# Startup order, named banks and the joints of pairs in an attention and expert kernel

## The chip, the core and the metric

The kernel runs on one core of a Trainium2 chip. The metric is the device time of one execution in microseconds (us). The core's engines run side by side, each through its own queue of instructions in a fixed order: TensorE (PE, matmuls; PEld its weight loads), VectorE (DVE), ScalarE (ACT), GpSimd (POOL) and SyncE (SP), which issues all the DMAs here. Results of TensorE go to PSUM, to which this kernel gives six tiles A0, A1, B0, B1, C0 and C1 (banks, called A, B and C in the rows) and the tile `psa`.

## The reference

Attention over chunks of 64 tokens, then a layer of four experts on its output. All is float32.

```python
scores = scale * q_c @ k_c.T          # 8 batches, 8 heads, 9 chunks of 64, head size 64
scores = scores - max(scores)
attn = exp(scores); attn = attn / (sum(attn) + 1e-09)
x = (attn @ v_c), reshaped to 4608 tokens x 512
p = domain_probs / (domain_probs.sum(-1) + 1e-09)
out = 0
for e in range(4):
    h = maximum(x @ w1[e], 0)          # 512 -> 1024
    out += p[:, e] * (h @ w2[e])       # 1024 -> 512
```

## The kernel before

**Numbers.** A float32 operand is split into a high part (a cast, on ScalarE) and a low part (the rest, on VectorE or GpSimd: L268 for x and weights, L463 and L637 for hidden values). A product is three matmuls for each k: high by high, low by high, high by low (L455). In the rows, xh and xl are the parts of x, wf a weight of the first layer (the name is also used for other buffers), hfh and hfl parts of hidden values and of second-layer weights.

**Tiling.** The tokens are nine blocks of 512. Block 0 goes alone, the other eight in four pairs. The hidden dimension and the experts are cut so that a block or a pair needs eight passes. Passes 0 to 7 are block 0: the startup is pass 0, `plain_pass` the rest. Passes 8 to 15 are the first pair (`first_pair_pass`), 16 to 39 the other three (`first_later_pass` is pass 16, `later_pass` the rest). A pass of a pair does its two layers not with eight products but with seven each, of sums and differences of the operands: p1 to p7 of a group. Groups g and h are the first layer, a and b the second, and the second layer of one pass is woven with the first layer of the next. The sums of x (`Tokens.sum1` to `sum4`, L405 and L420) are made at the last pass of the pair before: these are the joints of pairs, passes 23 to 24 and 31 to 32. The sums of the weights in the first pair (`w2.sum1` to `sum4`) are made in its passes, and `keep` stores their parts to memory for the pairs that follow. The sums of the hidden values (`sc.sum`, L628) have their high parts by L634 and low parts by L637. L683 adds products of the second layer to `acc`; L517 copies a product out of a bank (s), L656 and L622 combine such copies.

**Order.** Nothing is scheduled automatically. Each engine takes its instructions in the order in which the program issues them. A pass issues its products one after the other and behind step i the functions in `at[i]`, filled with `add(at, i, ...)`. What is handed on to the next pass stands in a list `late`. A bank is taken by name or, without a name, in turn. Who takes a tile that is still in use waits for the last user; this holds for a whole tile.

**The startup.** It loads the first block, keeps TensorE busy with matmuls of zeros (`keep_warm`, L857, into the tile `idle`), computes the attention of four tiles of 128 tokens (scores L815, softmax L182 to L187, weights L190 to L195, transposes L826, values L839, parts of x L265 and L268) and mixes in the first hidden products (`plain_hidden`). The sums of the softmax are also written to the tile `idle`:

```python
a_norm(es[t], sc[t], idle[:, 1, t * 2 * HG : (t + 1) * 2 * HG])
```

In the rows `idle` is called psa.

## Time and profile before

| | us |
|---|---|
| median of 3 runs | 1561.61 |
| lowest and highest | 1560.61, 1562.14 |
| the profiled execution | 1560.53 |
| its span | 1558.7 |
| TensorE busy in it | 1527.6 (98%) |
| VectorE busy | 918.0 (59%) |
| GpSimd busy | 883.2 (57%) |
| ScalarE busy | 574.3 (37%) |

The profile is one execution; the span is from its first to its last instruction. TensorE is near its whole span at work, so the waits that it still has lie in a few places, and the rows below are taken from there. The mean granted clock is 0.995 of full speed.

### The profile page before, as it was taken

The page shows a single profiled execution, that of the slowest core. Times are in us where ns is not written, and L with a number is a line of the kernel's source. Part 1 is how long each engine was busy: PE and PEld are TensorE (multiplying, and loading weights), DVE is VectorE, ACT ScalarE, POOL GpSimd, SP SyncE. Part 2 cuts the span into 40 slices and gives each one's busy share as a digit, 9 for nine tenths or more (in the row PEclk, how much of TensorE's full clock was granted, in tenths as well). Part 3 has the DMA queues.
Part 4 walks back from the last instruction along what each step waited for, and adds up shares of the span by engine and source line. Part 5 has one row for each costly group of instructions (what it writes and reads, how often), then busy time and mean ns, then how long its engine had stood idle before and what let it go on. Part 6 is the DMA issues. An engine that isn't in the chain of part 4 may idle for free.

```text
span 1558.7 us, 23407 instructions
## 1 busy us (share of the span) xinstructions
PE 1527.6 (98%) x8854; PEld 1240.8 (80%) x8854; DVE 918.0 (59%) x1288; ACT 574.3 (37%) x999; POOL 883.2 (57%) x664
## 2 busy tenths in 40 slices
PE   7999999999999999999999999999999999999998
PEld 5877877888888887888887778888887788888886
DVE  4444454444444456676777855666768745666665
ACT  3333444444433433333333434333333343333332
POOL 2333477676665715555555665555556755555554
PEclk8999999999999999999999999999999999999999
DMA  5345237877676676666665567676665576666654
GB/s 191 105 129 154 83 119 267 288 264 238 233 247 216 217 256 190 204 221 217 205 215 193 191 198 237 205 220 211 216 199 192 174 236 198 203 199 198 205 195 132
DMA packets 164831, 314.16 MB, mean 202 GB/s; under 512 B 14176, under 2 KB 79984, under 8 KB 164720
## 3 DMA queue, kind: packets, MB, share of 16 engines
q1 hardware_dynamic: 164720, 312.68, 61.8%
q8 instruction: 70, 1.15, 0.3%
q14 instruction: 41, 0.34, 0.1%
HBM read 244.39 MB, written 68.23 MB: 201 GB/s over the span
## 4 chain that ended last, share of the span: by engine, by line
PE 87%; DVE 4%; POOL 4%; DMA 3%; ACT 2%; issue 1%; SPq 0%; DVEq 0%; ACTq 0%; POOLq 0%
PE A L455 42%; PE C L455 25%; PE B L455 15%; PE psa L168 1%; PE psa L139 1%; POOL hfl L637 1%; PE psa L159 1%; DVE xl L268 1%; DMA w<-hfh 1%; DMA w<-wf 1%; POOL wf L268 1%; DMA wraw<-in_w 1%; DVE acc L683 1%; POOL xl L268 1%; PE psa L769 1%
## 5 line engine op out<-in xcount | busy, mean ns | idle before, releaser
L637 POOL TENSOR_TENSOR hfl<-wraw,hfh 128x512 fp32r<-128x512 f32 x288 | 388.8, 1369 | 209.0 <-ACT hfh L634 207.2
L455 PE MATMUL A<-xh,wf 128*128 128x512 f32 (+1 forms) x1112 | 382.9, 391 | 2.2 <-ACT s L517 2.0
L455 PE MATMUL A<-hfh,wf 128*128 128x512 f32 x768 | 271.1, 394 | 1.0 <-DVE acc L683 1.0
L634 ACT CAST hfh<-wraw 128x512 fp32r<-128x512 f32 x288 | 174.1, 622 | 216.6 <-POOL wraw L628 53.3
L455 PEld LDWEIGHTS A<-xh,wf 128*128 128x128 f32 x1112 | 208.2, 188 | 47.7 <-ACT s L517 2.9
L517 ACT COPY s<-A 128x512 f32<-128x512 f32 x192 | 112.8, 587 | 356.5 <-PE A L455 352.2
L455 PE MATMUL A<-xl,wf 128*128 128x512 f32 (+1 forms) x556 | 215.5, 388 | 2.3 <-POOL xl L268 2.3
L455 PE MATMUL C<-xh,wf 128*128 128x512 f32 (+1 forms) x584 | 201.4, 392 | 0.0
L455 PEld LDWEIGHTS A<-hfh,wf 128*128 128x128 f32 x768 | 144.2, 188 | 32.1 <-DVE acc L683 2.5
L683 DVE TENSOR_TENSOR acc<-A,acc 128x512 f32<-128x512 f32 x174 | 119.3, 685 | 79.6 <-PE A L455 78.6
L455 PE MATMUL A<-hfl,wf 128*128 128x512 f32 x384 | 149.8, 390 | 0.0
L455 PE MATMUL C<-hfh,wf 128*128 128x512 f32 x384 | 135.7, 395 | 3.2 <-DVE acc L683 2.9
L268 POOL TENSOR_TENSOR hfl<-wraw,hfh 128x512 fp32r<-128x512 f32 x64 | 85.9, 1370 | 85.5 <-ACT hfh L265 81.2
L455 PE MATMUL B<-xh,wf 128*128 128x512 f32 (+1 forms) x384 | 127.0, 384 | 1.3 <-DVE acc L751 1.3
L455 PEld LDWEIGHTS C<-xh,wf 128*128 128x128 f32 x584 | 109.6, 189 | 23.2
L268 POOL TENSOR_TENSOR wf<-wraw,wf 128x512 fp32r<-128x512 f32 x70 | 91.3, 1329 | 60.6 <-ACT wf L265 58.4
L455 PEld LDWEIGHTS A<-xl,wf 128*128 128x128 f32 x556 | 104.4, 188 | 23.8 <-POOL xl L268 3.1
L628 POOL TENSOR_TENSOR wf<-wraw,wf 128x512 f32<-128x512 f32 x23 | 29.7, 1293 | 165.1 <-DVE wf L622 165.1
L455 PE MATMUL C<-xl,wf 128*128 128x512 f32 (+1 forms) x292 | 113.3, 390 | 1.3 <-POOL xl L268 1.3
L683 DVE TENSOR_TENSOR acc<-C,acc 128x512 f32<-128x512 f32 x90 | 62.0, 690 | 58.9 <-PE C L455 54.6
L637 POOL TENSOR_TENSOR hfl<-wf,hfh 128x512 fp32r<-128x512 f32 x48 | 71.1, 1481 | 35.5 <-ACT hfh L634 35.5
L455 PEld LDWEIGHTS C<-hfh,wf 128*128 128x128 f32 x384 | 72.1, 188 | 20.1 <-DVE acc L683 4.9
(179 smaller groups left out, 2729.9 us busy)
## 6 DMA issues: line engine op xcount, KB each, us to landing
wf<-w SPq DMA_DIRECT2D x336, 512.0 KB, 4.1
wraw<-in_w SPq DMA_DIRECT2D x128, 256.0 KB, 3.6
w<-wf SPq DMA_DIRECT2D x112, 256.0 KB, 4.1
qk_in<-in_qk SPq DMA_DIRECT2D x32, 512.0 KB, 4.7
v_in<-in_v SPq DMA_DIRECT2D x32, 256.0 KB, 4.6
w<-hfl SPq DMA_DIRECT2D x32, 256.0 KB, 2.4
w<-hfh SPq DMA_DIRECT2D x32, 256.0 KB, 2.8
w<-hfh SPq DMA_DIRECT2D x48, 128.0 KB, 2.6
```

The lines of the kernel that those rows point to most:

```text
L139: nc.tensor.matmul(s["sc"][half, c, j], lhsT=s["x"][rows, g, 0, h], rhs=s["x"][rows, g, 1, h], start=True, stop=True,)
L159: nc.tensor.transpose(ps[:, j], s["e"][:, j].rearrange("p c k -> p (c k)"), ident)
L168: nc.tensor.matmul(av[half, c, j], lhsT=s["v"][rows, 2 * j + odd], rhs=s["pt"][rows, j, half], start=True, stop=True,)
L268: eng.tensor_tensor(out=t[1], in0=src, in1=t[0].bitcast(F32), op=ALU.subtract)
L455: nc.tensor.matmul(out, lhsT=lhs(k, a), rhs=rhs(k, b), start=first and i == 0, stop=last and i == len(parts) - 1, skip_group_check=not (fi ...
L517: nc.scalar.copy(out=t, in_=self.a)
L628: (eng or nc.vector).tensor_tensor(out=self.values[place, k], in0=self.values[a, k], in1=self.values[b, k], op=op)
L634: nc.scalar.copy(out=self.part(name, 0)[:, k], in_=self.values[name, k])
L637: (eng or nc.gpsimd).tensor_tensor(out=self.part(name, 1)[:, k], in0=self.values[name, k], in1=self.part(name, 0)[:, k].bitcast(F32), op=A ...
L683: nc.vector.tensor_tensor(out=acc[key], in0=src, in1=acc[key], op=ALU.add)
L769: nc.tensor.transpose(out_ps, acc[pair + 1, m + NK * s][:, j * P : (j + 1) * P], ident)
```

## The change

It has five parts. The startup gets an early Exp on one element, more matmuls of zeros, another order of the tiles' steps, and named banks. The last plain pass and the first pair get other banks for tiles (`TILE_BANKS`), and the first pair's pass 8 makes the parts of w2's sums later. Pass 16 makes the parts of t2 one step later. At the joints, x's sums move to other steps and partly to GpSimd. The low part of x's t4 is issued earlier in the next pass, and that of b22 is made on VectorE.

```diff
-WAITS = {"loads": 12, "softmax": 8}
+WAITS = {"loads": 12, "softmax": 14, "copy": 3}
...
-    TILE_BANKS = ("A0", "C0", "B0", "A1", "C1", "B1", "A1", "C1")
+    TILE_BANKS = ("A0", "B0", "C0", "A1", "C1", "B1", "A1", "C1")
...
-        sc[t] = bank().rearrange("p (h s) -> p h s", s=C)
+        sc[t] = bank(("A0", "A1", "C0", "C1")[t]).rearrange("p (h s) -> p h s", s=C)
...
-        w = bank().rearrange("p (j s) -> p j s", s=P)
+        w = bank(("B0", "B0", "B1", "B0")[t]).rearrange("p (j s) -> p j s", s=P)
...
-        av[t] = bank().rearrange("p (j s) -> p j s", s=P)
+        av[t] = bank(("B1", "A0", "A1", "B1")[t]).rearrange("p (j s) -> p j s", s=P)
...
         x_alloc(0)
+
+        nc.scalar.activation(out=small.tile([P, 1], F32, name="first"), in_=zeros[:, :1], func=AF.Exp)
         keep_warm(WAITS["loads"])
         start_scores(0)
         start_scores(1)
         keep_warm(WAITS["softmax"])
         start_softmax(0)
+        start_softmax(1)
         start_weights(0)
-        start_softmax(1)
-        for f, k in QUADS[:3]:
+        for f, k in QUADS[:2]:
             w1_split(f, k, nc.gpsimd)
         start_transpose(0)
-        w1_split(1, 1, nc.gpsimd)
+        keep_warm(WAITS["copy"])
         start_weights(1)
+        for f, k in QUADS[2:]:
+            w1_split(f, k, nc.gpsimd)
+        start_transpose(1)
         start_values(0)
         start_x(0)
-        start_transpose(1)
-        start_scores(2)
         start_values(1)
         start_x(1)
+        start_scores(2)
+        start_scores(3)
+        first = [0, 1]
         start_softmax(2)
         w_load(1, 0, 1, 0)
         w_load(1, 0, 1, 1)
         w2_split(0, 0)
-        start_scores(3)
-        first = [0, 1]
-        plain_hidden(0, first, order=RHS_LO_LAST)
+        start_softmax(3)
         start_weights(2)
+        plain_hidden(0, first, order=RHS_LO_LAST, name="B0")
         w2_split(0, 1)
-        plain_hidden(1, first, order=RHS_LO_LAST)
-        start_softmax(3)
+        plain_hidden(1, first, order=RHS_LO_LAST, name="B1")
         w2_split(1, 0)
-        plain_hidden(2, first, order=RHS_LO_LAST)
+        plain_hidden(2, first, order=RHS_LO_LAST, name="A0")
+        start_weights(3)
         start_transpose(2)
-        start_weights(3)
         w2_split(1, 1)
-        plain_hidden(3, first, order=RHS_LO_LAST)
+        plain_hidden(3, first, order=RHS_LO_LAST, name="C0")
         start_values(2)
         start_x(2)
         norm_probs()
-        o = tiles(0, 0, range(NT))
+        o = tiles(0, 0, range(NT), ("A0", "C0", None, None))
...
-        o = tiles(0, n, range(NT))
+        o = tiles(0, n, range(NT), ("C0", "C1", "A1", "B1") if ahead_of else None)
...
-            add(at, begin_w2 + 1 + i, lambda name=name: w2.hi(name), lambda name=name: w2.lo(name))
-            add(at, begin_w2 + 5 + i, lambda name=name: w2.keep(n, name))
+            later = 9 if begin_w2 else 1
+            add(at, later + i, lambda name=name: w2.hi(name), lambda name=name: w2.lo(name))
+            add(at, later + 4 + i, lambda name=name: w2.keep(n, name))
...
-            add(at, begin_w2 + 9 + i, lambda name=name: w2.hi(name), lambda name=name: w2.lo(name))
-            add(at, begin_w2 + 13 + i, lambda name=name: w2.keep(n, name))
+            later = 18 if begin_w2 else 9
+            add(at, later + i, lambda name=name: w2.hi(name), lambda name=name: w2.lo(name))
+            add(at, later + 4 + i, lambda name=name: w2.keep(n, name))
...
-        put(10, "t2", 0)
+        put(11, "t2", 0)
...
-        late = []
+        late, x_low = [], []
...
-            add(at, 0, x.sum1)
-            add(at, 4, x.sum3)
-            add(at, 7, x.sum2_apart)
+            add(at, 5, x.sum1)
+            add(at, 8, lambda: x.sum3(nc.gpsimd), lambda: x.sum2_apart(nc.gpsimd))
...
+            x_low = [lambda: x.lo("t4", nc.gpsimd)]
             late = [
-                (0, lambda: x.hi("b22")), (0, lambda: first_load(pair + 2)),
-                (7, lambda: x.lo("t4", nc.gpsimd)), (7, lambda: x.lo("b22", nc.gpsimd)),
+                (0, lambda: x.hi("b22")), (0, lambda: first_load(pair + 2)), (5, lambda: x.lo("b22")),
             ]
...
-        add(at, 4, lambda: sc.sum("t4", 1, nc.gpsimd))
+        add(at, 4, *x_low, lambda: sc.sum("t4", 1, nc.gpsimd))
```

In pass 8 `begin_w2` is 5, so w2's parts s1 and s2 went in at steps 6 and 7 and go in at 9 and 10, s3 and s4 at 14 and 15 and now 18 and 19. The last argument of `tiles` and the `name` of `plain_hidden` only say which bank is taken.

VectorE in the startup, the softmax of tiles 0 and 1 before the change (A is the bank with the scores of a tile, m its maxima, psa the tile `idle`):

```order
L182 TENSOR_REDUCE m_291<-A_249 128x8
L184 TENSOR_TENSOR A_249<-A_249,m_291 128x512
L190 TENSOR_REDUCE psa<-A_249 128x8
L191 TENSOR_SCALAR psa<-psa 128x8
L193 RECIPROCAL z_298<-psa 128x8
L195 TENSOR_TENSOR e<-A_249,z_298 128x512
L182 TENSOR_REDUCE m_301<-A_266 128x8
L184 TENSOR_TENSOR A_266<-A_266,m_301 128x512
L190 TENSOR_REDUCE psa<-A_266 128x8
L191 TENSOR_SCALAR psa<-psa 128x8
```

The same rows of VectorE with the change:

```order
L182 TENSOR_REDUCE m_299<-A_251 128x8
L184 TENSOR_TENSOR A_251<-A_251,m_299 128x512
L182 TENSOR_REDUCE m_303<-A_268 128x8
L184 TENSOR_TENSOR A_268<-A_268,m_303 128x512
L190 TENSOR_REDUCE psa<-A_251 128x8
L191 TENSOR_SCALAR psa<-psa 128x8
L193 RECIPROCAL z_310<-psa 128x8
L195 TENSOR_TENSOR e<-A_251,z_310 128x512
L190 TENSOR_REDUCE psa<-A_268 128x8
L191 TENSOR_SCALAR psa<-psa 128x8
```

The maxima of tile 1 now stand ahead of tile 0's sum (L190), and the two sums follow one another.

VectorE at the first joint, in pass 23, before the change (L405 and L420 are x's sums, xraw the pair's x, e and pt the sums kept apart):

```order
L405 TENSOR_TENSOR qk_in<-xraw 128x1024
L683 TENSOR_TENSOR acc_5805<-B_8127,acc_5805 128x512
L656 TENSOR_TENSOR B_8137<-B_8137,s_8119 128x512
L622 SCALAR_TENSOR_TENSOR wraw<-B_8137,s_5524 128x512
L405 TENSOR_TENSOR xraw<-xraw 128x2x512
L683 TENSOR_TENSOR acc_5865<-C_8163,acc_5865 128x512
L683 TENSOR_TENSOR acc_5887<-A_8101,acc_5887 128x512
L420 TENSOR_TENSOR e<-xraw,qk_in 128x512
L420 TENSOR_TENSOR pt<-xraw,qk_in 128x512
L683 TENSOR_TENSOR acc_5887<-C_8163,acc_5887 128x512
```

With the change, from the row that follows L628 on:

```order
L683 TENSOR_TENSOR acc_5816<-B_8136,acc_5816 128x512
L656 TENSOR_TENSOR B_8146<-B_8146,s_8128 128x512
L622 SCALAR_TENSOR_TENSOR wraw<-B_8146,s_5535 128x512
L683 TENSOR_TENSOR acc_5876<-C_8171,acc_5876 128x512
L405 TENSOR_TENSOR qk_in<-xraw 128x1024
L683 TENSOR_TENSOR acc_5898<-A_8112,acc_5898 128x512
L683 TENSOR_TENSOR acc_5898<-C_8171,acc_5898 128x512
```

Of the four sums one stays. It now stands behind the first L683 that reads bank C, where L405 of xraw stood ahead of it, and ahead of the two L683 that follow; the other three are gone from this engine.

GpSimd in the same pass with the change (before it, the last L628 followed the second L637 directly):

```order
L628 TENSOR_TENSOR wraw<-wraw 128x512
L637 TENSOR_TENSOR hfl_8134<-wraw,hfh_8132 128x512
L405 TENSOR_TENSOR xraw<-xraw 128x2x512
L420 TENSOR_TENSOR e<-xraw,qk_in 128x512
L420 TENSOR_TENSOR pt<-xraw,qk_in 128x512
L628 TENSOR_TENSOR wf_8252<-wraw,wf_8252 128x512
L637 TENSOR_TENSOR hfl_8299<-wraw,hfh_8297 128x512 x2
```

The three sums stand ahead of the sum of the hidden values L628.

GpSimd at the start of the next pass, 24, before the change (xl_8427 is the low part of x's t4, xl_8451 that of b22):

```order
L637 TENSOR_TENSOR hfl_8326<-wraw,hfh_8324 128x512
L637 TENSOR_TENSOR hfl_8364<-wf_8241,hfh_8362 128x512
L628 TENSOR_TENSOR wraw<-wraw 128x512
L637 TENSOR_TENSOR hfl_8469<-wraw,hfh_8467 128x512
L268 TENSOR_TENSOR xl_8427<-xraw,xh_8426 128x1024
L268 TENSOR_TENSOR xl_8451<-xraw,xh_8450 128x1024
L628 TENSOR_TENSOR wf_8581<-wraw,wf_8581 128x512
```

And with the change, where xl_8438 is the low part of t4:

```order
L637 TENSOR_TENSOR hfl_8393<-wraw,hfh_8391 128x512
L637 TENSOR_TENSOR hfl_8480<-wraw,hfh_8478 128x512
L637 TENSOR_TENSOR hfl_8337<-wraw,hfh_8335 128x512
L637 TENSOR_TENSOR hfl_8375<-wf_8252,hfh_8373 128x512
L268 TENSOR_TENSOR xl_8438<-xraw,xh_8437 128x1024
L628 TENSOR_TENSOR wraw<-wraw 128x512
L637 TENSOR_TENSOR hfl_8480<-wraw,hfh_8478 128x512
```

The low part of t4 went up past L628 and one L637; the other one is gone from this engine.

## Rows read from the trace of the kernel before

**Rows 1.** Windows: span, busy us (instructions) by engine, granted clock, DMA
```profile
13.40:20.20 6.80, 3.73 (x42) 2.88 (x42) 3.13 (x7) 3.74 (x8) 4.56 (x4) 0.50 0.72 245
...
593.70:597.10 3.40, 3.40 (x9) 2.64 (x8) 2.32 (x4) 1.51 (x3) 2.44 (x3) 0.50 0.19 75
...
850.00:906.00 56.00, 51.85 (x222) 40.77 (x221) 44.32 (x57) 21.26 (x33) 40.20 (x24) 1.00 0.61 201
...
0.00:1559.00 1559.00, 1527.65 (x8854) 1240.80 (x8854) 918.03 (x1288) 574.27 (x999) 883.15 (x664) 0.99 0.62 202
```

**Rows 2.** TensorE's waits: line, releaser, us in total, times, longest
```profile
PE C L455 <- DVE acc L683: 2.9, 2, 1.6
...
PE A L455 <- POOL xl L268: 2.3, 2, 1.2
...
PE A L455 <- ACT s L517: 2.0, 1, 2.0
...
PE A L455 <- DVE hfl L463: 1.6, 1, 1.6
...
PE C L455 <- POOL xl L268: 1.3, 2, 0.7
...
PE B L455 <- DVE acc L751: 1.3, 1, 1.3
...
PE C L455 <- DVE hfl L463: 0.7, 3, 0.3
```

**Rows 3.** Timeline of the startup: start, us, engine, line, operation, idle before
```profile
9.15 1.90 PE L857 MATMUL psa<-s 128*128 128x512 bf16 x8
...
9.18 1.28 ACT L187 ACT_TABLE_LOAD   x1 [9.18 <-DVE A L184]
...
11.16 0.70 DVE L190 TENSOR_REDUCE psa<-A 128x8 f32<-128x512 f32 x1 [2.06 <-ACT A L187]
...
13.18 0.89 PE L826 MATMUL B<-ident,e 128*128 128x128 f32 x4 [2.13 <-DVE e L195]
...
23.08 1.22 PE L455 MATMUL B<-xh,wf 128*128 128x256 f32 x8
...
28.71 0.63 PE L826 MATMUL C<-ident,e 128*128 128x128 f32 x4 [1.06 <-DVE e L195]
...
33.98 1.98 PE L839 MATMUL A<-s,ws 64*64 64x64 f32 x32 [3.21 <-issue]
...
35.89 1.11 PE L826 MATMUL B<-ident,pt 128*128 128x128 f32 x4
...
39.89 1.15 PE L839 MATMUL C<-s,ws 64*64 64x64 f32 x32
```

**Rows 4.** Timeline where tile 0 of pass 7 starts, TensorE and VectorE
```profile
214.32 0.39 PE L455 MATMUL A<-hfh,hfh 128*128 128x512 f32 x1
214.55 0.39 PE L455 MATMUL A<-hfl,hfh 128*128 128x512 f32 x1
...
214.43 1.41 DVE L463 SCALAR_TENSOR_TENSOR hfl<-C,hfh 128x512 fp32r<-128x512 f32 x2
```

**Rows 5.** Timeline of pass 16's start, ScalarE and VectorE
```profile
592.73 0.58 ACT L517 COPY s<-A 128x512 f32<-128x512 f32 x1
...
596.09 0.69 DVE L622 SCALAR_TENSOR_TENSOR wraw<-A,ws 128x512 f32<-128x512 f32 x1 [0.72 <-PE A L455]
```

**Rows 6.** Timeline of the first joint, VectorE and GpSimd
```profile
854.26 1.64 DVE L405 TENSOR_TENSOR xraw<-xraw 128x1024 f32<-128x1024 f32 x1
...
854.76 2.27 POOL L628 TENSOR_TENSOR wraw<-wraw 128x512 f32<-128x512 f32 x1
...
865.26 1.30 POOL L628 TENSOR_TENSOR wf<-wraw,wf 128x512 f32<-128x512 f32 x1 [5.82 <-DVE wf L622]
```

**Rows 7.** Timeline of the next pass's start, ScalarE and GpSimd
```profile
899.51 0.59 ACT L517 COPY s<-A 128x512 f32<-128x512 f32 x1 [1.11 <-PE A L455]
...
899.73 4.71 POOL L268 TENSOR_TENSOR xl<-xraw,xh 128x1024 fp32r<-128x1024 f32 x2
```

More of the change, by code (lines that the diff above doesn't have):

```diff
@@ L402, in __init__, with less @@
                     setattr(self, f"b{k + 1}{s + 1}", x[:, rows, toks])
-        def less(self, name, a, b, out):
-            nc.vector.tensor_tensor(
+        def less(self, name, a, b, out, eng=None):
+            (eng or nc.vector).tensor_tensor(
                 out=out, in0=getattr(self, a), in1=getattr(self, b), op=ALU.subtract
@@ L414, in sum2, with sum2_apart @@
             self.less("t2", "b22", "t1", self.b22)
-        def sum2_apart(self):
+        def sum2_apart(self, eng):
             self.t2 = [att.tile([P, SUB], F32, name=name) for name in ("e", "pt")]
             for k, t in enumerate(self.t2):
-                nc.vector.tensor_tensor(out=t, in0=self.b22[:, k], in1=self.t1[:, k], op=ALU.subtract)
+                eng.tensor_tensor(out=t, in0=self.b22[:, k], in1=self.t1[:, k], op=ALU.subtract)
         def sum4_apart(self):
@@ L432, in split2, with sum3 @@
                 split(nc.vector, t, [part[:, k] for part in xt[i]])
-        def sum3(self):
-            self.less("t3", "b22", "b12", self.b12)
+        def sum3(self, eng=None):
+            self.less("t3", "b22", "b12", self.b12, eng)
         def sum4(self):
@@ L479, in h_part, with plain_hidden @@
         return [t[:, k] for t in hs[s, i]]
-    def plain_hidden(f, tiles, alloc=True, order=BY_BLOCK):
+    def plain_hidden(f, tiles, alloc=True, order=BY_BLOCK, name=None):
         cols = slice(tiles[0] * P, (tiles[-1] + 1) * P)
@@ L484, in plain_hidden @@
             h_alloc(0, f)
-        out = bank()[:, : cols.stop - cols.start]
+        out = bank(name)[:, : cols.stop - cols.start]
         product(
@@ L1176, in later_pass @@
             add(at, i, f)
-        second_half(at, ahead[0])
+        second_half(at, ahead[0], ahead[2:])
         add(at, 12, lambda: sc.sum("t3", 0, nc.gpsimd))
@@ L1223, in later_pass, with second_half @@
                 f()
-        return (sc, left), late
-    def second_half(at, sc):
+        return (sc, left, *x_low), late
+    def second_half(at, sc, x_low=()):
         add(at, 0, lambda: sc.sum("t2", 1))
```

## Prediction

> **What bounds the kernel now.** I read the windows first [rows 1]. Over the whole run TensorE is busy 1527.65 of 1559 us, so nothing but its own waits and its clock can be won. Next came the table of what TensorE waits for [rows 2]. Its waits are few and each has a place: the startup, the step from block 0 to the first pair (about 222 to 249 us), one at 593 us, and the two joints of pairs (about 850 to 906, and the same again from 1182). One thing about these numbers: in a steady run a 512-column matmul starts every 0.23 us while its row lasts 0.39 [rows 4], so a wait between two such rows is 0.16 longer than its idle figure. I add this below. Last came the timeline at each place, to see what a wait's releaser itself had waited for.
>
> In the startup TensorE idles 2.13 us ahead of the transposes of tile 0, 1.06 ahead of those of tile 2 and 3.21 ahead of the values of tile 2 [rows 3]. While the granted clock is down, work takes longer: the window from 13.4 to 20.2 us was granted 0.50 [rows 1], the lower level (1.2 GHz); it was granted just behind the wait of 2.13, which ends at 13.18. The values of tile 2, after the wait of 3.21, took 1.98 us, those of tile 3 only 1.15; transposes took 1.11 at 35.89 and 0.63 at 28.71 [rows 3].
>
> **A, the startup.** The early Exp takes the table load (1.28 us, 9.18) out of tile 0's chain. I cost that at nothing, because of what the sum at 11.16 is: it writes its result into the tile `idle` (psa in the rows), the same tile into which the warm matmuls write, and the order makes it follow the last of them. Before, eight of them end at 11.05 (9.15 + 1.90), just ahead of the sum, whose row names the Exp as what came last [rows 3]. The change makes them fourteen. At 0.24 us each (1.90 for 8) they end near 12.4, so tile 0's sum moves from 11.16 to about 12.5, and its transposes, 2.02 us behind the sum in the rows, from 13.18 to about 14.5. After them (0.63) come three more warm matmuls (0.7), and tile 1's sum now follows those: about 15.8, transposes of tile 1 about 17.9. Then transposes 0.63, values of two tiles and scores of two tiles at about 1.1 each: plain hidden 0 at about 22.9 against 23.08, a gain of 0.2 only.
>
> The gain is behind it. The softmax of tiles 2 and 3 is issued ahead of the hiddens and the weights of tile 2 ahead of hidden 0, so the waits of 1.06 and 3.21 should go: 4.3. The low clock that follows the second of them goes too: 0.83 on the values, 0.48 on the transposes, 1.3 together. A new wait comes: the transposes of tile 2 take bank B1, which hidden 1 has just filled, and wait for its low part, which stands on VectorE behind the weights of tile 2; I estimate 0.6, one short VectorE instruction. So −0.2 − 4.3 − 1.3 + 0.6 = −5.2. Against this stands one more low stretch: TensorE still waits about 2.1 twice (12.4 to 14.5, 15.8 to 17.9), and the wait of 2.13 in the rows was followed by 0.50 from 13.4 on. If the stretch falls on the transposes of tile 1 and the values of tile 0, it costs 0.48 + 0.83 = 1.3. I take it: **−3.9**, bounds −2.5 and −6.
> The Trainium skill, "TensorE: Matmul & The Clock Gate", Part 1, says that the clock follows how busy the engine has been lately. The windows agree. By that rule the longer warm run might as well keep the clock up, and the startup would then give 5.2, not 3.9.
>
> **B, the banks between passes 7 and 8.** The wait of 1.3 for VectorE's `acc` add on bank B (1.43 with the 0.16) goes, since the last tiles of block 0 no longer hold B0. But tile 0 now takes C0, in which hidden 2 still lies: its low part, the first of two in a row, ends near 215.1 (214.43 + half of 1.41), and TensorE starts the tile at 214.32 [rows 4]. The new wait is about 0.8. Sum **−0.6**, bounds +0.8 (the old wait only moves to another bank) and −1.4.
>
> **C, the sums of w2 later in pass 8.** The wait of 1.6 for `hfl` on bank A (1.76) comes from the activations of the hiddens, which stand on ScalarE behind casts of w2's sums. With those casts three to four steps later the activation waits for its bank alone; I leave 0.25 for the rest of the chain, an estimate: **−1.5**, bounds 0 and −1.76. What is moved past: the casts, GpSimd's low parts and the stores that `keep` queues on SP. These stores are first read a pair later, and GpSimd's queue gets the same work three steps later; I cost that at nothing. If that cover fails, one low part on GpSimd is late, 1.3 [rows 6], and C is nearly gone, which is its lower bound.
>
> **D, the first pair's tile banks.** Three waits on C for `hfl`, 0.7 together, with 0.16 each 1.2, in passes 8, 9 and 14: the second tile takes B0 instead of C0, and they go. **−1.2**, bounds 0 and −1.2.
>
> **E, put t2 a step later in pass 16.** TensorE waits 2.0 (2.16) for a COPY on ScalarE at 592.73 [rows 5], which stands behind a cast that itself waited for VectorE. Behind the wait a window of 3.4 us had the clock 0.50, and nine matmuls were started in it [rows 1], for which 0.23 each would be 2.0: 1.4 lost. With the cast behind the COPY, the COPY still needs its own bank; about 0.9 us of wait is left (its own 0.58 and the ways there and back), which would probably not bring the clock down. That gives up to 2.16 + 1.4 − 0.9 = 2.7. But the next step needs bank A from VectorE's L622, at 596.09 in the rows, and the high part that is now later; a wait of some 1 to 2 us comes there instead. **−1.0**, bounds 0 and −2.7.
>
> **F, x's sums away from VectorE at the joint.** Product a3 waits for `acc<-C` [rows 2], which stands in VectorE's queue behind L405 at 854.26 (1.64) [rows 6]. That L405 goes to GpSimd; the one that stays follows behind this `acc<-C`, ahead of later ones that TensorE does not yet want. So both waits (2.9 together, 3.2 with 0.16 each) go. GpSimd gets the three sums, as one of 1024 columns and two of 512. A 512-column sum takes 1.30 there when nothing disturbs it, and L268 of 1024 columns 2.36 (4.71 for 2) [rows 6, 7], so 5.0 us. GpSimd was idle 5.82 us ahead of 865.26 [rows 6], so they lie beside TensorE's work. **−3.2**, bounds −2 and −3.2.
> L628 at 854.76, beside VectorE's L405 with two SBUF inputs, took 2.27, and the same form at 865.26 took 1.30 [rows 6]. At that ratio the sums take 8.7, and the 2.9 past the gap delay L628 and its casts. What VectorE runs in the gap reads a PSUM bank each time, so I go by 1.30.
> The Trainium skill, "SBUF — State Buffer", section "SBUF: two separate sides", says that a VectorE operation with two SBUF inputs and a GpSimd operation hold a common port pair one at a time, each for its whole length. The two rows agree, and it speaks against this part: by it, any such VectorE operation that remains in the gap adds its length.
>
> **G, x's low parts.** The waits for `xl` (2.3 and 1.3 in all, four of them over both joints, 4.24 with 0.16 each) go: the low part of t4 is issued ahead, and that of b22 on VectorE. The price is a new queue. On GpSimd the low part of t4 (2.36) now stands ahead of sum L628, so the cast that reads the sum on ScalarE is about 2.4 later, and the COPY at 899.51 behind that cast too [rows 7]. The COPY can be some 1 us late before g4 wants its bank; I estimate a wait of 0.75 to 1.9 each time and take 1.3: 4.24 − 2.6 = **−1.6**, bounds 0 and −2.8.
>
> **The sum:** −3.9 − 0.6 − 1.5 − 1.2 − 1.0 − 3.2 − 1.6 = −13.0. The profiled execution took 1560.53 us (span 1558.7), 1.1 below the median of the runs. On the median 1561.61 this gives **1548.6 us**.
>
> **The rivals.**
> 1. The startup gains nothing. For it: both waits of 2.1 stay, and the warm matmuls delay the sums more than the table load saved. Against it: the two later waits lose their cause. Without A: 1552.5.
> 2. The joints' waits only move (F and G come to nothing): the sums take 8.7, and the COPY waits behind the cast. For it: the 2.27 at 854.76. Against it: VectorE's work in the gap. 1548.6 + 4.8 = 1553.4.
> 3. The clock does not fall in the startup, and E gives all its 2.7: 1548.6 − 1.3 − 1.7 = 1545.6.
> 4. The other side: GpSimd becomes the bound at the joints. It is busy 40.2 of 56 us there [rows 1]; with the sums at 8.7 that is 49. It decides if a product needs one of GpSimd's low parts before the queue has recovered: then the sums' 8.7 stands on the path at both joints, 17.4, and F and G are lost: 1548.6 + 4.8 + 17.4 = 1570.8. Against it: 7 us are left, and the first reader of a sum is issued ten steps later.
>
> **How the numbers follow.** My forecast gets 0.44, rival 1 0.17, rival 2 0.12, rival 3 0.19, rival 4 0.04. The forecast's own terms move it by about 3 either way. The range 1544 to 1553.5 holds the forecast nearly whole with rivals 1, 2 and 3. What a measurement of this kernel can tell from no change is about 0.2%, 3.1 us; rivals 1 to 3 are all faster by more. Several terms at their poor bounds at once would end within it: the last 0.04. Slower is rival 4: 0.04.
>
> **What would show it.** Right: transposes of tile 0 near 14.5 and tile 0 of block 0 near 31.5 (a row of 512 columns out of `hfh,hfh`), no wait of 3 us in the startup; no wait for `acc` on B between passes 7 and 8, one below 1 us for C0 at the first tile of pass 7; no `acc` wait on C and no `xl` wait at the joints, but one for a COPY of L517 near 900; GpSimd's three sums between 857 and 866 in about 5 us. Wrong: a clock of 0.50 in more of the startup than one stretch, sums of over 2 us each on GpSimd, or a new wait of over 2 us behind the COPY.

## The result and the profile after

| | before | after |
|---|---|---|
| median, us | 1561.32 (4 runs) | 1546.62 (4 runs) |
| lowest and highest | 1560.61, 1562.14 | 1546.44, 1547.34 |
| profiled execution | 1560.53 | 1546.54 |
| its span | 1558.7 | 1544.8 |
| TensorE busy in it | 1527.6 | 1524.5 |

The ratio is 0.9907, with a 95% interval from 0.9889 to 0.9924: 14.7 us less. The forecast was 1548.6, 13.0 less.

What TensorE waits for in the changed kernel behind the startup (line, releaser, us in total, times, longest):

```profile
PE A L455 <- ACT s L517: 3.7, 3, 1.5
...
PE B L455 <- POOL hfl L637: 1.2, 1, 1.2
...
PE C L455 <- DVE hfl L463: 0.7, 1, 0.7
...
PE A L455 <- DVE wraw L622: 0.6, 1, 0.6
PE A L455 <- DVE hfl L463: 0.6, 1, 0.6
```

Of the rows of [rows 2] those for `acc` on C, for `xl` and for `acc` on B are gone. The three waits for `hfl` on C are gone too; the one that stands there now is the first tile of pass 7, which takes C0. The wait of 1.6 for `hfl` on A is gone, and the 0.6 that stands there now comes 30 matmuls later. New are also 1.2 for GpSimd's `hfl`, 0.6 for L622, and two of the three waits for a COPY. In the startup the wait of 2.13 for the weights of tile 0 stays and one as long for those of tile 1 is new; those of 1.06 and 3.21 [rows 3] are gone, and with them one of 3.06 for the copy (L830) of tile 0, which those rows do not show.

Where the time came from is best seen by following the same instruction through both traces. These are starts of the same instruction in the two profiled executions, in us (L749 and L751 take a tile of block 0 or of the first pair into `acc` on VectorE, L517 is a COPY on ScalarE):

| place | before | after | after less before | since the last row |
|---|---|---|---|---|
| L749 of tile 0, block 0 | 40.00 | 34.61 | −5.39 | −5.39 (A) |
| L751, first tile of pass 7 | 221.80 | 216.44 | −5.36 | 0.03 |
| L751, its last tile | 229.97 | 223.77 | −6.20 | −0.84 (B) |
| L749, tile 0 of pass 8 | 257.15 | 249.83 | −7.32 | −1.12 (C) |
| L517, first of pass 10 | 315.63 | 307.43 | −8.20 | −0.88 (D) |
| L517, first of pass 16 | 576.08 | 567.38 | −8.70 | −0.50 (D) |
| L517, in pass 18 | 652.76 | 643.71 | −9.05 | −0.35 (E) |
| L517, pass 23 | 850.96 | 841.95 | −9.01 | 0.04 |
| L517, behind a3 | 866.41 | 855.50 | −10.91 | −1.90 (F) |
| L517, pass 24 | 908.69 | 897.13 | −11.56 | −0.65 (G) |
| L517, pass 30 | 1150.50 | 1138.94 | −11.56 | 0.00 |
| L517, second a3 | 1191.65 | 1178.42 | −13.23 | −1.67 (F) |
| L517, pass 33 | 1267.57 | 1253.71 | −13.86 | −0.63 (G) |

The row of pass 8 holds two things that happen to cancel: its L749 came 0.45 late in VectorE's own queue (the next one is 7.77 earlier than before), and the first of D's three waits lies ahead of it. Followed by TensorE's own matmuls (L455), C is −1.0 and D −1.5.

The startup after, in the same columns as [rows 3]:

```profile
8.90 3.19 PE L857 MATMUL psa<-s 128*128 128x512 bf16 x14
...
9.34 0.58 ACT L187 ACTIVATE A<-A 128x512 f32<-128x512 f32 x1 [7.10 <-DVE A L184]
...
12.21 0.70 DVE L190 TENSOR_REDUCE psa<-A 128x8 f32<-128x512 f32 x1 [1.65 <-PE psa L857]
...
14.23 0.63 PE L826 MATMUL B<-ident,e 128*128 128x128 f32 x4 [2.13 <-DVE e L195]
...
17.64 1.09 PE L826 MATMUL B<-ident,pt 128*128 128x128 f32 x4 [2.13 <-DVE pt L195]
...
18.66 1.97 PE L839 MATMUL B<-s,qk_in 64*64 64x64 f32 x32
...
23.36 1.21 PE L455 MATMUL B<-xh,wf 128*128 128x256 f32 x8
...
28.07 0.66 PE L826 MATMUL B<-ident,e 128*128 128x128 f32 x4
...
31.58 0.48 PE L455 MATMUL A<-hfh,hfh 128*128 128x512 f32 x1
```

The first row of tile 0 of block 0, the last of these, was before:

```profile
36.66 0.78 PE L455 MATMUL B<-hfh,hfh 128*128 128x512 f32 x1
```

The fourteen warm matmuls end at 12.09 (8.90 + 3.19), and tile 0's sum follows at 12.21, with PE as what it waited for, though its Exp was done at 9.92. The transposes come at 14.23 and 17.64, both with a wait of 2.13. The low clock falls within the second: the values of tile 0 take 1.97. From hidden 0 on there is no wait of note: 23.36 to 31.58 at tile 0 of block 0, where before it was 23.08 [rows 3] to 36.66.

The windows (columns as in [rows 1]) show the clock at the lower level, 1.2 GHz, for one stretch of the startup (before there were two, of 6.8 and 3.4 us), and both engines that share the work of a joint:

```profile
17.10:20.50 3.40, 2.86 (x38) 2.56 (x40) 0.39 (x1) 0.59 (x1) 1.47 (x2) 0.50 0.38 128
838.00:894.00 56.00, 53.82 (x234) 43.01 (x233) 45.93 (x57) 22.64 (x36) 44.09 (x27) 1.00 0.61 199
```

GpSimd is busy 44.09 of 56 us there, VectorE 45.93. GpSimd's three sums lie in its gap, and 0.64 of the gap is left ahead of L628 (where 5.82 had been, [rows 6]):

```profile
848.78 2.40 POOL L405 TENSOR_TENSOR xraw<-xraw 128x1024 f32<-128x1024 f32 x1
...
851.13 1.31 POOL L420 TENSOR_TENSOR e<-xraw,qk_in 128x512 f32<-128x512 f32 x1
...
852.40 1.31 POOL L420 TENSOR_TENSOR pt<-xraw,qk_in 128x512 f32<-128x512 f32 x1
...
854.35 1.30 POOL L628 TENSOR_TENSOR wf<-wraw,wf 128x512 f32<-128x512 f32 x1 [0.64 <-DVE wf L622]
```

They took 5.0 us, as estimated. What VectorE keeps of x's sums, L405, ran ahead of them, beside GpSimd's L628 at 844.51, which took 2.29 there instead of 1.30.

The wait of 0.6 for `hfl` on A in pass 8 comes from a load:

```profile
244.13 0.62 ACT L265 CAST wf<-wraw 128x512 fp32r<-128x512 f32 x1 [3.15 <-DMA wraw<-in_w]
...
246.02 0.50 PE L455 MATMUL A<-hfh,hfh 128*128 128x512 f32 x1 [0.59 <-DVE hfl L463]
```

The cast on ScalarE waited 3.15 for the load of a weight. The activation that makes the hidden values stands behind it (244.65), VectorE's low part behind that (245.28), and the product behind that. The new wait of the next pass of the joint, 24:

```profile
884.37 2.31 DVE L268 TENSOR_TENSOR xl<-xraw,xh 128x1024 fp32r<-128x1024 f32 x1
...
885.53 3.40 POOL L268 TENSOR_TENSOR xl<-xraw,xh 128x1024 fp32r<-128x1024 f32 x1
...
888.89 1.28 POOL L628 TENSOR_TENSOR wraw<-wraw 128x512 f32<-128x512 f32 x1
...
890.73 0.58 ACT L517 COPY s<-A 128x512 f32<-128x512 f32 x1
...
891.36 0.50 PE L455 MATMUL A<-xh,wf 128*128 128x512 f32 x1 [1.47 <-ACT s L517]
```

The low part of t4 on GpSimd takes 3.40, not the 2.36 of [rows 7], since it starts while VectorE's low part of b22 runs; L628 stands behind it, the COPY behind the cast of that sum, and TensorE waits 1.47.

### The profile page after: what moved, and what is told of

Its sections match the earlier page's. It is cut to its first block, busy times and chain, and to the rows that moved or that the text cites. A ratio compares the mean times of both kernels' runs of the same rounds, so it can differ in the third digit from the quotient of the medians.

```text
span 1544.8 us, 23430 instructions
## 1 busy us (share of the span) xinstructions
PE 1524.5 (99%) x8863; PEld 1239.6 (80%) x8863; DVE 915.7 (59%) x1284; ACT 574.8 (37%) x1000; POOL 888.5 (58%) x668
## 4 chain that ended last, share of the span: by engine, by line
PE 78%; POOL 3%; DVE 2%; ACT 1%; issue 1%; DMA 0%; DVEq 0%; SPq 0%; POOLq 0%; ACTq 0%
PE A L455 41%; PE C L455 22%; PE B L455 12%; POOL hfl L637 2%; PE psa L168 1%; PE psa L139 1%; DVE xl L268 1%; PE psa L159 1%; PE psa L769 1%; DVE acc L683 1%; POOL wraw L628 0%; POOL xl L268 0%; DVE wraw L628 0%; ACT hfh L634 0%; ACT xh L265 0%
## 5 line engine op out<-in xcount | busy, mean ns | idle before, releaser
L637 POOL TENSOR_TENSOR hfl<-wraw,hfh 128x512 fp32r<-128x512 f32 x288 | 386.1, 1360 | 207.6 <-ACT hfh L634 205.7
L455 PE MATMUL A<-xh,wf 128*128 128x512 f32 (+1 forms) x1112 | 382.4, 390 | 3.9 <-ACT s L517 3.7
L455 PE MATMUL A<-hfh,wf 128*128 128x512 f32 x768 | 271.2, 394 | 1.6 <-DVE acc L683 1.0
L455 PEld LDWEIGHTS A<-xh,wf 128*128 128x128 f32 x1112 | 207.8, 188 | 49.8 <-ACT s L517 5.5
L517 ACT COPY s<-A 128x512 f32<-128x512 f32 x192 | 112.7, 587 | 347.2 <-PE A L455 343.0
L455 PE MATMUL A<-xl,wf 128*128 128x512 f32 (+1 forms) x556 | 214.8, 387 | 0.0
L455 PE MATMUL C<-xh,wf 128*128 128x512 f32 (+1 forms) x584 | 201.1, 391 | 0.0
L455 PEld LDWEIGHTS A<-hfh,wf 128*128 128x128 f32 x768 | 144.2, 188 | 33.1 <-DVE acc L683 2.5
L683 DVE TENSOR_TENSOR acc<-A,acc 128x512 f32<-128x512 f32 x174 | 119.3, 686 | 77.3 <-PE A L455 76.4
L455 PE MATMUL A<-hfl,wf 128*128 128x512 f32 x384 | 149.7, 390 | 0.0
L455 PE MATMUL C<-hfh,wf 128*128 128x512 f32 x384 | 135.4, 394 | 0.2
L268 POOL TENSOR_TENSOR hfl<-wraw,hfh 128x512 fp32r<-128x512 f32 x64 | 86.0, 1371 | 83.4 <-ACT hfh L265 79.8
L455 PEld LDWEIGHTS C<-xh,wf 128*128 128x128 f32 x584 | 109.1, 188 | 23.2
L455 PE MATMUL B<-xh,wf 128*128 128x512 f32 (+1 forms) x384 | 126.9, 383 | 0.0
L268 POOL TENSOR_TENSOR wf<-wraw,wf 128x512 fp32r<-128x512 f32 x70 | 91.4, 1331 | 55.9 <-ACT wf L265 53.6
L455 PEld LDWEIGHTS A<-xl,wf 128*128 128x128 f32 x556 | 104.3, 188 | 20.7
L628 POOL TENSOR_TENSOR wf<-wraw,wf 128x512 f32<-128x512 f32 x23 | 29.8, 1294 | 156.3 <-DVE wf L622 156.3
L455 PE MATMUL C<-xl,wf 128*128 128x512 f32 (+1 forms) x292 | 112.8, 388 | 0.0
L683 DVE TENSOR_TENSOR acc<-C,acc 128x512 f32<-128x512 f32 x90 | 62.1, 691 | 60.7 <-PE C L455 54.8
L637 POOL TENSOR_TENSOR hfl<-wf,hfh 128x512 fp32r<-128x512 f32 x48 | 71.2, 1483 | 35.5 <-ACT hfh L634 35.5
L455 PEld LDWEIGHTS C<-hfh,wf 128*128 128x128 f32 x384 | 72.1, 188 | 16.3 <-DVE acc L683 1.1
```

What stands on the lines that cost most here:

```text
L268: eng.tensor_tensor(out=t[1], in0=src, in1=t[0].bitcast(F32), op=ALU.subtract)
L455: nc.tensor.matmul(out, lhsT=lhs(k, a), rhs=rhs(k, b), start=first and i == 0, stop=last and i == len(parts) - 1, skip_group_check=not (fi ...
L517: nc.scalar.copy(out=t, in_=self.a)
L628: (eng or nc.vector).tensor_tensor(out=self.values[place, k], in0=self.values[a, k], in1=self.values[b, k], op=op)
L637: (eng or nc.gpsimd).tensor_tensor(out=self.part(name, 1)[:, k], in0=self.values[name, k], in1=self.part(name, 0)[:, k].bitcast(F32), op=A ...
L683: nc.vector.tensor_tensor(out=acc[key], in0=src, in1=acc[key], op=ALU.add)
```

## The experiments

Single executions differ by 1 us and more through the startup alone (the last section). So each experiment is read at its place, by the difference of the same VectorE and ScalarE instructions from the kernel that it was made of, as in the table above. "Earlier" and "later" are such differences.

**The startup alone**, on the kernel before: `WAITS`, `startup` and the named banks of its helpers.

```diff
-WAITS = {"loads": 12, "softmax": 8}
+WAITS = {"loads": 12, "softmax": 14, "copy": 3}
...
         start_softmax(0)
+        start_softmax(1)
         start_weights(0)
-        start_softmax(1)
...
```

> The kernel before with the change's startup alone. Theory (the trace of after, where tile 1 of block 0 ends 5.4 us earlier than before): about 5.4 us less than before, 1555.9 in the median, nearly all of it between hidden 0 and tile 0 of block 0, and all other waits of before stay. Rival (the startup's gain needs the named banks of the later parts, since the turn of the unnamed banks shifts): a new wait in passes 1 to 8 takes more than 1 us of it back.

It ran in 1557.59 us, beside 1560.60 for the kernel before. Tile 0 of block 0 is 3.80 earlier, not 5.4, and nothing of it is lost up to pass 8. In this run the low clock held for 6.8 us (17.4 to 24.2) instead of 3.4. In pass 8 the wait for `hfl` was 1.9, the clock fell behind it (242.7 to 246.1), and 1.3 was lost there. So the startup stands by itself; its size differs from run to run, here by 1.6 us, with the low clock held twice as long.

**The sums in tiles of their own.** The warm matmuls and the softmax sums of the startup no longer share a tile.

```diff
-        a_norm(es[t], sc[t], idle[:, 1, t * 2 * HG : (t + 1) * 2 * HG])
+        a_norm(es[t], sc[t], small.tile([P, 2 * HG], F32, name=f"sums{t}"))
```

> After, with the startup's four softmax sums in tiles of their own instead of the tile that the warm matmuls write. Theory (the sums of tiles 0 and 1 stand behind the warm matmuls): transposes of tile 0 from 14.23 to about 12.6, those of tile 1 from 17.64 to about 14.6, hidden 0 from 23.36 to about 19.6 at full clock, so about 3 us less than after, and up to 4.2 if the low clock stretch at 17.1 to 20.5 goes too: 1542.4 to 1543.6. Rival (the loads set the startup): hidden 0 stays at about 23 and nothing is gained.

1543.03 us. The startup of this kernel:

```profile
9.42 3.19 PE L857 MATMUL psa<-s 128*128 128x512 bf16 x14
...
10.86 0.68 DVE L190 TENSOR_REDUCE sums<-A 128x8 f32<-128x512 f32 x1
...
12.86 0.63 PE L826 MATMUL B<-ident,e 128*128 128x128 f32 x4 [0.25 <-DVE e L195]
...
14.64 0.63 PE L826 MATMUL B<-ident,pt 128*128 128x128 f32 x4 [0.51 <-ACT wf L265]
...
19.84 1.21 PE L455 MATMUL B<-xh,wf 128*128 128x256 f32 x8
```

and the window of it:

```profile
5.60:44.00 38.40, 35.96 (x428) 30.37 (x426) 22.94 (x44) 16.19 (x32) 12.54 (x10) 1.00 0.50 168
```

The sum starts at 10.86 while the warm matmuls run (9.42 to 12.61), the two waits of 2.13 become 0.25 and 0.51, the clock stays at full speed throughout, and hidden 0 starts at 19.84 instead of 23.36, although the scores of tile 1 had waited 1.18 for their load. Tile 0 is 3.8 earlier than after. So after it was the shared tile that set the startup, and not the loads. (With the tile gone they come next: tile 0's sum now starts right behind the maxima of tile 1 on VectorE, which had waited for that load.)

**No early Exp**, so that the table load stands in tile 0's chain again.

```diff
-        nc.scalar.activation(out=small.tile([P, 1], F32, name="first"), in_=zeros[:, :1], func=AF.Exp)
```

> After without the early Exp, so that the table load of 1.28 us stands again ahead of tile 0's Exp. Theory (tile 0's sum waits for the fourteenth warm matmul, not for the Exp): the sum starts at 12.2 as in after, the time is that of after within 0.3 us. Rival (the Exp sets it): the sum starts 1.3 us later and the time is 1.3 us above after.

1548.08 us, above what the theory expected. The rows:

```profile
8.95 1.28 ACT L187 ACT_TABLE_LOAD   x1 [8.95 <-DVE A L184]
...
9.39 3.20 PE L857 MATMUL psa<-s 128*128 128x512 bf16 x14
...
10.24 0.58 ACT L187 ACTIVATE A<-A 128x512 f32<-128x512 f32 x1
...
12.70 0.70 DVE L190 TENSOR_REDUCE psa<-A 128x8 f32<-128x512 f32 x1 [1.77 <-ACT wf L265]
```

The table load delays the Exp to 10.24, the Exp is done at 10.82, and the sum starts at 12.70, just behind the last warm matmul (12.59). (The cast that its row names, L265, ended then as well, but writes nothing that the sum reads; after, the sum started while that cast still ran.) From the start of the warm matmuls to the sum it is 3.31 us, the same as after (8.90 to 12.21). So the early Exp brings nothing here. The 1.3 us by which tile 0 came later have two other causes in this run: the warm matmuls started 0.49 later, since tile 1's scores waited 0.92 for their load, and the low clock held for 6.8 us (16.3 to 23.1). Of the rest of the kernel 0.8 came back in pass 8 and 1.1 was lost at the first joint, both by what the last section tells.

**Eight warm matmuls** instead of fourteen.

```diff
-WAITS = {"loads": 12, "softmax": 14, "copy": 3}
+WAITS = {"loads": 12, "softmax": 8, "copy": 3}
```

> After with eight warm matmuls ahead of the softmax instead of fourteen. Theory (the last of them sets tile 0's sum, A): the sum and the transposes of tile 0 and all that follows come 1.2 to 1.3 us earlier relative to the loads; if the clock falls earlier because TensorE then idles from 10.8 on, low stretches cost up to 2.5 us of it back. Rival (the Exp or the loads set the sum): nothing moves.

1545.56 us.

```profile
9.27 1.67 PE L857 MATMUL psa<-s 128*128 128x512 bf16 x7 [0.16 <-issue]
...
11.06 0.70 DVE L190 TENSOR_REDUCE psa<-A 128x8 f32<-128x512 f32 x1 [0.47 <-PE psa L857]
...
13.08 0.63 PE L826 MATMUL B<-ident,e 128*128 128x128 f32 x4 [2.13 <-DVE e L195]
```

(The record of the first of the eight is missing; by the spacing of the others, 0.22, it started near 9.05.) The sum starts about 2.0 behind the first warm matmul instead of 3.31, the 1.3 that the theory said, and the transposes of tile 0 come at 13.08, although the loads were late. The low clock held from 14.1 to 20.9, and tile 0 of block 0 was 0.39 earlier than after. The six matmuls are time in front of the sum; what they may have saved of the clock is not more.

**Tile 0 of the last plain pass in another bank.**

```diff
-        o = tiles(0, n, range(NT), ("C0", "C1", "A1", "B1") if ahead_of else None)
+        o = tiles(0, n, range(NT), ("A1", "C0", "C1", "B1") if ahead_of else None)
```

> After with the last plain pass's tiles in banks A1, C0, C1, B1, so that tile 0 does not wait for hidden 2's low part. Theory (term B of the prediction): that wait of 0.84 us goes and the time is 0.8 us less than after. Rival (VectorE is late there in any case): the wait comes back a little later, at the first products of the next pass, and the time stays within 0.3 us.

1545.86 us; 0.74 us is gained between the start of the pass and its last tile, and it is kept (0.84 to the end). B's new wait was real, and another bank takes it away.

**The parts of w2's sums early again**, in pass 8 of the changed kernel.

```diff
-            later = 9 if begin_w2 else 1
+            later = 6 if begin_w2 else 1
...
-            later = 18 if begin_w2 else 9
+            later = 14 if begin_w2 else 9
```

> After with the parts of w2's sums in pass 8 at the steps of before (6, 7 and 14, 15). Theory (C: the casts ahead of the hiddens' activations on ScalarE make the wait): the wait for hfl on bank A at 246 us grows from 0.6 to about 1.7, and if the clock falls behind it by one stretch of 3.4 us, 1.1 to 2.5 us more time than after. Rival (the new banks took that wait away as well): no more than 0.3 us.

1552.57 us. The wait, and the window behind it:

```profile
PE A L455 <- DVE hfl L463: 2.4, 1, 2.4
```

```profile
242.60:246.00 3.40, 3.40 (x9) 2.64 (x8) 2.07 (x5) 2.69 (x5) 0.00 (x0) 0.50 1.07 396
```

The wait is 2.4, longer than the 1.6 of the kernel before and than the 1.7 expected, nine matmuls start in 3.4 us behind it, and 3.4 us are lost there in all. So the early casts do make the wait, and beside the new banks the late ones are worth more than the 1.0 to 1.1 of the table. The table's figure is itself a low one. The wait of 0.6 that comes from the weight load is not among the waits of eight of the ten runs made of after, this one included; that gave 0.4 to 0.8 back. And in the two other runs that hold before's pass 8 (the startup alone, x's sums alone) its wait was 1.9 and 1.8, and the clock fell behind it, as it had not before.

**t2's parts early again** in pass 16.

```diff
-        put(11, "t2", 0)
+        put(10, "t2", 0)
```

> After with t2's parts in pass 16 at step 10 again. Theory (E): the wait for the COPY grows from 0.7 to 2.0, one low clock stretch of 3.4 us follows (1.4), and two smaller waits behind it (0.6 and 1.2) shrink, so 0.6 us more than after, as the two traces differ there. Rival (prediction's bound): all of it is lost again, 2.7 us more.

1549.61 us, with a startup 1.8 later and 1.2 lost at the first joint (see below, L622). At pass 16 it loses 0.60, the number of the theory, but not by its way, so the agreement is luck. The wait for the COPY grew to 1.94 and that for L622 went, as said; but the wait for GpSimd's `hfl` grew from 1.24 to 1.51 instead of shrinking, and the clock did not fall, though in the kernel before it fell behind a wait of 1.95 for the same COPY [rows 1, 2].

**The first pair's tile banks of before.**

```diff
-    TILE_BANKS = ("A0", "B0", "C0", "A1", "C1", "B1", "A1", "C1")
+    TILE_BANKS = ("A0", "C0", "B0", "A1", "C1", "B1", "A1", "C1")
```

> After with the first pair's tile banks of before (second tile in C0, third in B0). Theory (D): waits on C for hfl of 0.6 or so return in passes 8 and 14 and a small one in pass 9, about 1.4 us more than after behind the startup. Rival: other banks are free by then and nothing returns.

1548.59 us.

```profile
PE C L455 <- DVE hfl L463: 1.1, 3, 0.7
```

One of these three is the first tile of pass 7, as after. The other two have returned, in passes 8 and 14, 0.2 each; the one of pass 9 has not. They cost the matmuls behind them 0.5 each, 1.0 together, of the 1.4 expected.

**x's sums alone**, on the kernel before.

```diff
-            add(at, 0, x.sum1)
-            add(at, 4, x.sum3)
-            add(at, 7, x.sum2_apart)
+            add(at, 5, x.sum1)
+            add(at, 8, lambda: x.sum3(nc.gpsimd), lambda: x.sum2_apart(nc.gpsimd))
```

> The kernel before with only x's sums moved as in the change (sum1 to step 5, the other three to GpSimd at step 8); the low parts stay as before. Theory (F is 1.6 us at each joint and G the rest): the wait for acc on C goes at both joints, those for xl stay at 1.2 and 0.7, so about 3.2 us less than before. Rival (GpSimd's 5 us of sums delay its later low parts): the waits for xl grow, gain below 1.5 us.

1559.86 us, with a startup that was 1.7 later and 1.3 lost in pass 8, where the clock fell. The first joint gives 1.9, the second 1.7. The waits for `xl` of the first joint are those of before:

```profile
PE A L455 <- POOL xl L268: 1.1, 1, 1.1
PE C L455 <- POOL xl L268: 0.7, 1, 0.7
```

So F is 3.6 us by itself, and its sums cost GpSimd nothing that TensorE sees.

**The low part of t4 behind the sum.**

```diff
-        add(at, 4, *x_low, lambda: sc.sum("t4", 1, nc.gpsimd))
+        add(at, 4, lambda: sc.sum("t4", 1, nc.gpsimd), *x_low)
```

> After, with the low part of x's t4 on GpSimd behind the sum t4,1 instead of ahead of it. Theory (G: the wait of 1.5 for the COPY at 890.7 comes from that sum, which stands behind the low part of 3.40): the wait goes at both joints and at most 0.25 comes back as a wait for xl, so the time is 2.6 to 3.2 us less than after, besides what the startup's clock does. Rival (the low part is then late for its own matmuls, as it was before): waits for xl of about 1 us at each joint, gain below 1 us.

1545.45 us. The second joint gains 1.34, the first 0.20, so 1.5 in all where the theory had 2.6 to 3.2. The longest of TensorE's waits at the first joint:

```profile
PE A L455 <- DVE wraw L622: 1.2, 1, 1.2
```

The wait for the COPY is gone at both joints, as the theory said. But at the first joint L622 made it wait 1.2, where it had not been among the waits after. That is another thing, and the next experiment was for it.

**What L622 waits for.** After and the run with t2 early hold the same work at this place of the first joint. First the changed kernel, GpSimd and VectorE:

```profile
872.09 4.40 POOL L637 TENSOR_TENSOR hfl<-wraw,hfh 128x512 fp32r<-128x512 f32 x2 [0.17 <-ACT hfh L634]
...
874.12 1.21 DVE L268 TENSOR_TENSOR xl<-xraw,xh 128x1024 fp32r<-128x1024 f32 x1
...
875.26 0.68 DVE L622 SCALAR_TENSOR_TENSOR wraw<-A,s 128x512 f32<-128x512 f32 x1
```

and the other:

```profile
874.05 3.31 POOL L637 TENSOR_TENSOR hfl<-wraw,hfh 128x512 fp32r<-128x512 f32 x2 [0.17 <-ACT hfh L634]
...
876.10 2.35 DVE L268 TENSOR_TENSOR xl<-xraw,xh 128x1024 fp32r<-128x1024 f32 x1
...
878.37 0.68 DVE L622 SCALAR_TENSOR_TENSOR wraw<-A,s 128x512 f32<-128x512 f32 x1
...
879.11 0.50 PE L455 MATMUL A<-xh,wf 128*128 128x512 f32 x1 [1.22 <-DVE wraw L622]
```

One operation, L268 of 1024 columns with two SBUF inputs, takes 1.21 or 2.35, and GpSimd's two low parts beside it take 4.40 or 3.31: one of the two engines waits for the other. Which one it will be cannot be seen ahead: in all eighteen passages of the next sentence the record of L268 starts within 0.02 us of that of GpSimd's second low part. L622, for which TensorE waits, is behind L268. In the nine runs with this order (after, and all made of it but the last two of this list), each with two joints, L268 took 2.35 six times of eighteen; after it did so at neither joint.
The Trainium skill, "SBUF — State Buffer", section "SBUF: two separate sides", says that the first of the two to start holds the shared ports for its whole instruction. The rows agree in that one of the two takes its usual time and the other about that much longer; which was first, they do not show.

```diff
-            add(at, 25, lambda: x.hi("t3"), lambda: x.lo("t3"))
-            add(at, 26, lambda: x.hi("t4"))
+            add(at, 25, lambda: x.hi("t3"))
+            add(at, 26, lambda: x.lo("t3"), lambda: x.hi("t4"))
```

> After with the low part of x's t3 one step later at the joints (26 instead of 25), so that on VectorE the operation L622, for which TensorE waits there, stands ahead of it. Theory (that low part of 1024 columns has two SBUF inputs and takes 1.2 or 2.4 us at one and the same place, by whether it or GpSimd's low part starts first): L622 waits for it no more, and TensorE's wait for L622 (0.3 or 1.4 with the row's 0.16) is gone at both joints whichever starts first; the wait for the COPY of 1.5 may grow by up to 0.4 as a result. Rival (L622 is late by itself): the wait stays at one or both joints.

1550.30 us. The wait for L622 is gone at both joints. But the wait for the COPY grew, and the clock fell behind it, which had not been expected:

```profile
PE A L455 <- ACT s L517: 1.9, 1, 1.9
```

```profile
892.30:895.60 3.30, 3.30 (x10) 2.53 (x9) 2.20 (x4) 0.00 (x0) 0.36 (x1) 0.50 0.20 47
```

Each joint lost 1.65 us. The step alone only hands the time on to the next wait, and the low clock comes on top.

**All four together:** the sums apart, the low part of t4 behind the sum, the bank of tile 0, t3 later.

> After with the startup's sums in tiles of their own, the low part of t4 behind the sum, the last plain pass's tiles in A1, C0, C1, B1, and the low part of t3 one step later. Theory (the gains add: 3.8 with the clock at full speed in the startup, 2.7, 0.8, and 0.3 to 1.4 at each joint): 8 to 9 us less than after, about 1538. Rival (the joints' waits only change places): 4.6 less, about 1542.

1539.87 us (median of 4 runs, 1539.04 to 1542.02), ratio to before 0.9858 (0.9841 to 0.9874), 21.7 us less, and 6.8 less than after. What is left of the waits that the edits were for:

```profile
PE C L815 <- issue: 1.8, 1, 1.8
...
PE A L455 <- POOL xl L268: 1.2, 2, 0.6
...
PE A L455 <- ACT s L517: 0.7, 1, 0.7
```

The startup gave 2.8 (in this run the last scores of tile 3 came 1.76 late, put down to no instruction), the bank 0.7, each joint about 1.3. The 1.3 is no more than the low part behind the sum alone gave at the second joint. With the sum out of the way, t3 later costs nothing; it takes the wait for L622 away, and the wait for `xl` that comes instead is 0.6. Between the two theories' 1538 and 1542 it lies in the middle.

## Why the prediction held, and where its sizes were off

The mechanisms were right; the sum was 0.9 us short of the traces' 13.9. The steps miss by more than that in both directions, so that it came so near is in part luck.

| step | forecast | measured in the table |
|---|---|---|
| A, startup | −3.9 | −5.4 |
| B, banks of pass 7 | −0.6 | −0.8 |
| C, w2's parts later | −1.5 | −1.1 |
| D, tile banks | −1.2 | −1.4 |
| E, t2 later | −1.0 | −0.35 |
| F, x's sums | −3.2 | −3.6 |
| G, x's low parts | −1.6 | −1.3 |

**A** held in each of its turns: the sum behind the fourteenth matmul (12.2, forecast 12.5), the transposes at 14.2 and 17.6 (14.5 and 17.9), and one low stretch of 3.4 us (in the seven other profiles of this startup it was 6.8). Tile 0 came at 31.6, beside the 31.5 of the forecast's signs; but 31.5 is 36.66 less the 5.2 without the clock's price, and the −3.9 that went into the sum makes it 32.8, so that agreement is luck. That the shared tile sets it was shown by taking it away: 3.8 us. Two terms were mis-sized. The wait of 0.6 for hidden 1's low part did not come (28.07, no idle time in the row). And the values and scores were counted at 1.1 us each, the length of a row, while at full clock one starts a little less than 1.0 behind the other; with transposes that were 0.3 earlier and a low stretch that cost about 1.0 (beside the startup with the sums apart) and not 1.3, hidden 0 came at 23.4, not the 24.2 that 22.9 and 1.3 make. The size differs from run to run on both sides: in those seven profiles its tile 0 came 0.2 to 1.8 later, and in the one other profile of the startup of before 1.7 later. Single pairs give anything from −3.6 to −7.1, the averages of both −5.2; the forecast's −3.9 lies at the poor end.
The Trainium skill, "TensorE: Matmul & The Clock Gate", Part 1, lets the clock follow how busy the engine has lately been. The runs agree: with fourteen warm matmuls and with eight the clock fell to 0.50, and it stayed up in the two kernels whose startup has no wait of 2 us. What the forecast made of the rule, that the longer warm run might do, did not come true.

**B** and **D** held; the bank experiments gave 0.7 to 0.9 and about 1.0, the second less than the table since the wait of pass 9 did not come back. D was priced low: a wait costs the matmuls behind it 0.3 more than its idle figure, not 0.16 (0.30 idle in pass 8, 0.60 lost), since the row after it starts late too (0.34 behind instead of 0.23, at 245.94 of before).

**C** is the right cause with a size that depends on the rest: 1.1 in the table, 3.4 when it is undone beside the new banks, 1.4 or so of that the clock. The wait that the forecast priced went whole (nothing is left of it, where 0.25 had been kept back), 1.9 with its row; what took 0.9 of it back is the wait for a weight load, which the forecast did not have.

**E** is the step with the worst size: a third. The low clock behind the wait went (nothing of 0.50 there after), and with the shorter wait for the COPY that gave 2.8, as forecast (2.7). But two waits behind it took 2.4 back, not the 1.7 that the −1.0 allows: 0.6 for L622, which the forecast named, and 1.2 for GpSimd's `hfl`, which it did not.

**F** held, with 5.0 us of sums in a gap of 5.6. Rival 2's price of 8.7 did not come, since VectorE ran nothing with two SBUF inputs beside them; where it did, beside L628 at 844.51, that price was paid (2.29). Rival 4 needed GpSimd to have no room; it was busy 44 of 56 us.

**G** held in its mechanism, and the wait for the COPY is 1.4 to 1.5 at each joint, as estimated (1.3). It was avoidable: one line's order gave 1.34 at the second joint. At the first it took the wait away too, but L622 took 1.1 of it back. The wait has two parts: the low part of t4 itself, which the forecast had at 2.36, and about 1.0 that it loses to VectorE's low part of b22; which of them decides was not tested.

What stays open: what decides whether the low stretch of the startup is 3.4 us or 6.8; which of the startup's edits the gain is due to, since its order and its banks were only tried together (the early Exp gave nothing, and the six matmuls cost time); and why D's wait of pass 9 did not come back.

## What to carry to other kernels

Filler work that is meant to keep an engine's clock up must share nothing with the work that it covers: a tile used by both is a wait, here 3.5 us for the hidden products behind it. A wait that is taken away in a full pipeline exposes the next in line, so read which queue the new order makes longer, and put the operation that another engine waits for ahead of one that nobody does. Start one operation behind the other, not the length of its row, when you add up a chain of pipelined matmuls. And take the size of a step from more than one execution of either kernel: one pair of profiles gave the startup 5.4 us, others 3.6 to 7.1.

## What the runs showed that had not been expected

**The clock differs from run to run.** One and the same startup was granted 0.50 for 3.4 us in the profile of after and for 6.8 us in the seven others, where its first tile came 0.2 to 1.8 us later. Part of that is the load of tile 1's queries and keys, for which its scores waited up to 1.7 us. The startup of before differs as much: in x's sums alone its first tile came 1.7 later.

**A toss between two engines.** L268 takes 1.21 or 2.35 us at the same place of the same program, by which of VectorE and GpSimd waits for the other, and moves the end by 1.1 us or so.

**The same wait brought the clock down in one run and not in another.** The wait for the COPY in pass 16 was 1.95 before, 1.94 with the startup alone and 1.95 with x's sums alone, and a stretch of 0.50 followed each time; with t2 early it was 1.94, and none followed.

**A load of weights reaches TensorE through ScalarE's queue.** In pass 8 a cast that waits for a weight stands ahead of an activation. In after and nine of the runs made of it the cast waited 2.1 to 3.3 us, and the matmuls that need the activation came on time or up to 0.9 late.
